# Strassen's seven products for the outer products of the second layer, with SiLU's values kept in float32

## The chip, the cores and the metric

The kernel runs on 1 core of one Trainium2 chip. The metric is the device time of one execution in microseconds; a version's time is the median of its runs. Engines are named as in the profile: PE is TensorE's matrix multiply and PEld its weight load, DVE is VectorE, ACT is ScalarE, POOL is GpSimd, SP is SyncE, which issues the DMAs here.

## The reference, cut to what matters

An attention stage (4 batches, 8 heads, pooled queries) gives x with 2304 rows (tokens) and 512 columns. Two layers follow, one behind the other:

```python
h = x @ w_in                # 2304x512 @ 512x2048
g = h * np.cos(h)
x = g @ w_out               # 2304x2048 @ 2048x512
h = x @ w_in2
g = h * (1.0 / (1.0 + np.exp(-h)))
out = g @ w_out2            # float32, the output
```

The attention's inputs are float32, the weights of both layers float64. This case is about the second layer, and in it about `g @ w_out2`.

## The kernel before, in words

Every product is made in float16 with a high and a low part of each operand: hi·hi, hi·lo and lo·hi are summed in PSUM, so a product of float32 quality costs three matmuls. Matmuls are at most 128 by 128 of weights by 512 columns.

**Tokens.** The second layer works on nine blocks of 256 tokens (`NB = 2 * B + 1`), a block's values lying as 128 partitions (a sixteenth of d_ff) by 256 tokens. `NF` is 16, the number of such slices f.

**First product of a block** (`g1_unit`, L527): for each f, 12 matmuls of 128x256 into half a PSUM bank; two f share a bank `h`, and there are two such banks. `g1_evac` (L540, ACT) takes two f at once out of PSUM with SiLU into `hk`, a float32 tile of four f with two buffers. After each fourth f, `g_silu` (L574, L575, DVE) scales `hk` and splits it into `gt`, float16 high and low. Four `gt` tiles, in the room of the first layer's weights, allow for four blocks (`TAIL_G`).

**Second product** (`g2_unit2`, L607): tokens are the stationary operand, 128 at a time; the weights' 512 columns stream. For each f there are 6 matmuls of 128x512: two halves of the block by three terms. So a block has 96 of them, in two banks `o0` and `o1`. `y_evac2` (L617, DVE) multiplies both banks by the scales into `osb`, and SP writes the rows out (L622).

**Order.** The program text issues the first product of blocks 0 to 2 alone, and from block 3 on one f of the first product, then one f of the second product of three blocks before. Behind the last first product, three blocks of second products remain. A planner puts the instructions of each engine in order before the run, by the text's order and by what its own timeline takes to be ready; it may bring later work forward where an engine would be idle.

**Weights.** `weight_steps` handles w_in2 and w_out2 as eight pieces each. A piece is loaded in three buffers (L177, SP), its float64 words are made into float32 (L206 to L218; ACT, DVE), a scale is found over the partitions with a tiny matmul on PE (L96), and the piece is split into high and low (L238, L239 on ACT, L240 on POOL). Three pieces of w_out2 are split before the second layer begins and five in its first 45 us. The POOL part of such a piece is one subtraction of 128x1024.

The blocks of the second layer are loaded (L871), measured and split (L890, L891) one ahead; they too find their scale with the matmul at L96, which has two PSUM buffers in `ps_m`.

Of the kernel before, what the change touches and what calls it, by code (L numbers as in the profile page):

```python
# [11 lines left out]
F32 = mybir.dt.float32  # L12
# [28 lines left out]
GT = 3  # L41
TAIL_G = 4


@with_exitstack
def attention_moe_moe_kernel(ctx, tc, q, k, v, w_in1, w_out1, w_in2, w_out2, out):
# [83 lines left out]
    def run_all(g):  # L130
        for _ in g:
            pass
# [10 lines left out]

    def new_w(tag, npc):
        w = Weights()
        w.npc = npc
        w.half = False
        for nm in ("si", "ui", "so", "uo"):
            setattr(w, nm, const.tile([128, npc], F32, name=nm + tag))
        w.uoT = const.tile([128, NC], F32, name="uoT" + tag)  # L150
        w.kg = const.tile([128, 1], F32, name="kg" + tag)
        w.ug = const.tile([128, 1], F32, name="ug" + tag)
        return w

    def weight_steps(w, srcs, stage, pspool, eng, nsub, bufs, ahead, wt_bufs=WT_BUFS):
# [16 lines left out]
        def more():  # L172
            if todo:
                kind, p, h = todo.pop(0)
                c, n = shape(kind)
                st = stage.tile([128, c, n, z], I32 if wide else F32, tag="wst", name="wst", bufs=bufs)
# [14 lines left out]
        def decode(kind, p):  # L191
            c, n = shape(kind)
            s, u = (w.si, w.ui) if kind == "i" else (w.so, w.uo)
            s, u = s[:, p:p + 1], u[:, p:p + 1]
            m = small.tile([128, nsub], F32, name="wm", tag="wm", bufs=3)
            sts = [staged.pop(0) for _ in range(nsub)]
            ts = []
            for h, st in enumerate(sts):
                if not wide:
                    ts.append(st[:, :, :, 0])  # L200
                    absmax(m[:, h:h + 1], ts[-1], AX.XY)
                    yield
                    continue
                t = stage.tile([128, c, n], F32, tag="wt", name="wt", bufs=wt_bufs)
# [16 lines left out]
                ts.append(st.bitcast(F32)[:, :, :, 1])  # L221
# [5 lines left out]
            for _ in early(scale_steps(m1, pspool(), (s, u), 14, wide), P_CH):  # L227
                pass
            decoded.append(ts)
            yield  # L230

        def write(kind, p):
            c, n = shape(kind)
            hw, lw = (w.ih, w.il) if kind == "i" else (w.oh, w.ol)
# [8 lines left out]
            if (kind, p) == ("i", npc - 1):  # L243
# [3 lines left out]
                nc.vector.tensor_reduce(out=w.ug, in_=w.ui, axis=AX.X, op=ALU.max)  # L247
                nc.vector.tensor_scalar(out=w.kg, in0=w.kg, scalar1=2.0**-15, scalar2=None, op0=ALU.mult)
                nc.vector.tensor_scalar(out=w.ug, in0=w.ug, scalar1=2.0**12, scalar2=None, op0=ALU.mult)

# [6 lines left out]

        r = npc // NC
        for e in range(r):
# [273 lines left out]
    def g1_evac(mp, w, blk, f, first):  # L533
        if f % 2 == 0:
            return
        g = f * w.npc // NF
        if f % 4 == 1:
            blk.hk = mp.p.tile([128, 4, GW], F32, tag="hk", name="hk", bufs=NB_HK)
        o = blk.hk[:, (f % 4) - 1:(f % 4) + 1, :]
        nc.scalar.activation(  # L540
# [58 lines left out]

    def g2_unit2(w, blk, f, pool):  # L600

        if f == 0:
            blk.y = [pool.tile([128, DM], F32, tag="o%d" % i, name="o") for i in range(2)]
        gh, gl = blk.g[f // 4]
        for i in range(2):
            for e, (gt, wt) in enumerate(((gh, w.oh), (gh, w.ol), (gl, w.oh))):
                nc.tensor.matmul(  # L607
                    blk.y[i], gt[:, f % 4, i * 128:(i + 1) * 128], wt[:, f, :],
                    start=(f == 0 and e == 0), stop=(f == NF - 1 and e == 2),
                )  # L610

    def y_evac2(W2, pool, blk, dsts):
        cy = y_scale(W2, blk.u, W2.uo, "cy0")
        for i in range(2):
            o = pool.tile([128, DM], F32, tag="x32_%d" % i, name="osb")
            np_ = W2.npc
            nc.vector.tensor_tensor(  # L617
                out=o.rearrange("p (c n) -> p c n", c=np_), in0=blk.y[i].rearrange("p (c n) -> p c n", c=np_),
                in1=cy.rearrange("p (c n) -> p c n", n=1).to_broadcast([128, np_, DM // np_]), op=ALU.mult,
            )  # L620
            for dst, p0, n in dsts[i]:
                nc.sync.dma_start(out=dst, in_=o[p0:p0 + n, :])  # L622


    if True:
        W1 = new_w("1", 8)
        alloc_w(W1, wpool, "1")
        ydr = [dram.tile([128, NC * GW], F32, name="ydr%d" % i) for i in range(2 * B + 1)]
        xrem = wpool.tile([128, B, NP * D], F32, name="xrem")

# [10 lines left out]
        state.psw = ps_h  # L641
        W2 = new_w("2", 8)
        state.credit = 0.0
# [148 lines left out]
        for n, (b, j) in enumerate(pairs):  # L792
# [13 lines left out]
            else:  # L806
                at.src_stack.close()
                w2st = moe_stack.enter_context(tc.tile_pool(name="w2st", bufs=1, reuse_waits="tile"))
                wgen2 = weight_steps(W2, (w_in2, w_out2), w2st, lambda: state.psw, nc.sync, 1, W2_BUFS, 1, 1)
# [52 lines left out]

        alloc_w(W2, w2p, "2")
        state.psw = ps_m
# [32 lines left out]
        def y_consts(yb):  # L897
            yb.blk.c = x_scale_consts(W2, yb.s, yb.u, False)
            yb.blk.u = yb.u
            yb.blk.gt = wpool.tile([128, 2, NF, GW], F16, tag=("ih1", "il1", "oh1", "ol1")[yb.n % TAIL_G], name="gt", bufs=1)  # L900

# [6 lines left out]
        while not W2.half:  # L908
            next(wgen2)

        def out_dst(n):
# [13 lines left out]
        cur = yb.blk  # L925
        pend = []

        def second():
            blk, ff, nn = pend.pop(0)
            g2_unit2(W2, blk, ff, ps_o)  # L930
            if ff == NF - 1:
                y_evac2(W2, wpool, blk, out_dst(nn))

        gen = None
        for n in range(NB):
            nyb = y_load(n + 1) if n + 1 < NB else None
            gen = y_split(nyb) if nyb else None
            for f in range(NF):
                g1_unit(W2, cur, f)
                g1_evac(state.mp, W2, cur, f, False)  # L940
                if f % 4 == 3:
                    g_silu(cur, f)
                pend.append((cur, f, n))
# [3 lines left out]
                if len(pend) > (TAIL_G - 1) * NF:  # L947
                    second()
            if n == TAIL_G - 2:
                run_all(wgen2)  # L950
            if gen is not None:
                run_all(gen)
            if nyb:
                y_consts(nyb)
                cur = nyb.blk
        while pend:
            second()
        ctx.enter_context(moe_stack)
# [30 lines left out]
```

## Time and profile before

| | us |
|---|---|
| median of 3 runs | 1407.86 (1405.83 to 1409.97) |
| the profiled execution's own time | 1411.62 |
| its span, first to last instruction | 1409.8 |
| second layer, first matmul to last matmul | 1021.0 to 1404.6 |

The profile has a page (busy time per engine, 40 slices of the span, the chain that ended last, groups of instructions) and a trace that can be asked for any stretch. In a group's row, "x36 | 46.2, 1282 | 0.9" means 36 instructions, 46.2 us busy in sum, 1282 ns mean, and 0.9 us that the engine sat idle just before them. Matmuls are pipelined: the mean of one is longer than the distance from one to the next, so the pace is read from runs of them in the chain.

### The profile page before, as it was taken

The page shows a single profiled execution, that of the slowest core. Times are in us where ns is not written, and L with a number is a line of the kernel's source. Part 1 is how long each engine was busy: PE and PEld are TensorE (multiplying, and loading weights), DVE is VectorE, ACT ScalarE, POOL GpSimd, SP SyncE. Part 2 cuts the span into 40 slices and gives each one's busy share as a digit, 9 for nine tenths or more (in the row PEclk, how much of TensorE's full clock was granted, in tenths as well). Part 3 has the DMA queues.
Part 4 walks back from the last instruction along what each step waited for, and adds up shares of the span by engine and source line. Part 5 has one row for each costly group of instructions (what it writes and reads, how often), then busy time and mean ns, then how long its engine had stood idle before and what let it go on. Part 6 is the DMA issues. An engine that isn't in the chain of part 4 may idle for free.

```text
span 1409.8 us, 24849 instructions
## 1 busy us (share of the span) xinstructions
PE 1162.9 (82%) x10020; PEld 852.0 (60%) x10020; DVE 996.4 (71%) x1848; ACT 767.5 (54%) x907; POOL 567.2 (40%) x296
## 2 busy tenths in 40 slices
PE   1465356787988778898889889979989999999998
PEld 0243233475676556666667678868878766666643
DVE  7999997778777888977999885997776323223110
ACT  3686487668777678876788775553363111111100
POOL 1577276535755466645666563552321000000000
PEclk9976568699999989998999999999999999999999
DMA  7799789987799999978899964441330000000001
GB/s 232 192 239 209 188 155 204 202 171 135 154 201 174 202 194 211 177 151 181 152 209 184 214 131 91 151 119 46 90 105 32 16 31 30 16 16 16 1 30 30
DMA packets 493074, 186.16 MB, mean 132 GB/s; under 512 B 433056, under 2 KB 467872, under 8 KB 492960
## 3 DMA queue, kind: packets, MB, share of 16 engines
q1 hardware_dynamic: 492960, 184.59, 61.7%
q8 instruction: 78, 1.28, 0.4%
q14 instruction: 36, 0.29, 0.1%
HBM read 66.58 MB, written 9.44 MB: 54 GB/s over the span
## 4 chain that ended last, share of the span: by engine, by line
PE 36%; DVE 25%; ACT 9%; issue 8%; DMA 7%; POOL 2%; SPq 2%; ACTq 0%; DVEq 0%; POOLq 0%
PE h L527 14%; PE o L607 13%; DVE sc L410 5%; PE y L586 5%; DMA hlT<-hl 3%; DVE tt L553 2%; DVE tt L552 2%; POOL hl L429 2%; PE sp L391 2%; ACT hl L424 2%; SPq L431 2%; PE pv L442 2%; DVE gh L567 1%; DVE tt L562 1%; DVE vt L311 1%
## 5 line engine op out<-in xcount | busy, mean ns | idle before, releaser
L429 POOL TENSOR_TENSOR hl<-sc,hl 128x1152 f16<-128x1152 f32 x144 | 367.8, 2563 | 189.9 <-ACT hl L424 110.8
L391 PE MATMUL sp<-kT,qT 128*128 128x512 f16 (+1 forms) x768 | 197.6, 375 | 111.2 <-DVE sc L410 86.5
L527 PEld LDWEIGHTS <-ih 128*128 128x128 f16 x2304 | 225.8, 99 | 64.6 <-issue 12.5
L410 DVE TENSOR_SCALAR_CACHE_REDUCE sc<-sp,psu 128x512 f32<-128x512 f32 (+1 forms) x288 | 229.2, 807 | 40.2 <-PE sp L391 38.8
L540 ACT ACTIVATE hk<-h,ca 128x512 f32<-128x512 f32 x144 | 97.7, 682 | 255.0 <-PE h L527 251.0
L418 ACT ACTIVATE sc<-sc,nb 128x1152 f32<-128x1152 f32 x144 | 180.3, 1252 | 95.2 <-DVE nb L415 80.6
L442 PE MATMUL pv<-vt,hlT 128*128 128x130 f16 (+1 forms) x1440 | 197.2, 239 | 39.6 <-DMA hlT<-hl 33.3
L527 PE MATMUL h<-ys,ih 128*128 128x256 f16 x1152 | 194.8, 273 | 2.9 <-ACT hk L540 2.7
L442 PEld LDWEIGHTS <-hlT 128*128 128x128 f16 (+1 forms) x1440 | 148.6, 111 | 71.0 <-DMA hlT<-hl 45.4
L527 PE MATMUL h<-xT,ih 128*128 128x256 f16 x1024 | 187.1, 276 | 4.7 <-ACT hk L540 3.9
L446 PE MATMUL pv<-vt,hlT 128*128 128x65 f16 (+1 forms) x1440 | 189.5, 209 | 0.0
L607 PE MATMUL o<-oh,gt 128*128 128x512 f16 x576 | 187.9, 379 | 1.0 <-ACT oh L238 0.6
L391 PEld LDWEIGHTS <-qT 128*128 128x128 f16 x768 | 77.9, 110 | 179.2 <-issue 137.1
L424 ACT ACTIVATE hl<-sc 128x1152 f16<-128x1152 f32 x144 | 165.5, 1157 | 18.5 <-DMA xT<-xn 8.9
L586 PE MATMUL y<-gl,oh 128*128 128x256 f16 x576 | 159.4, 277 | 3.7 <-POOL gl L568 3.7
L586 PE MATMUL y<-gh,oh 128*128 128x256 f16 x576 | 159.8, 277 | 2.5 <-ACT y L595 1.7
L586 PE MATMUL y<-gh,ol 128*128 128x256 f16 x576 | 159.7, 277 | 0.0
L527 PE MATMUL h<-ys,il 128*128 128x256 f16 x576 | 157.0, 273 | 0.0
L446 PEld LDWEIGHTS <-hlT 128*128 128x128 f16 (+1 forms) x1440 | 143.7, 108 | 16.2 <-issue 6.7
L527 PE MATMUL h<-xT,il 128*128 128x256 f16 x512 | 141.5, 276 | 0.0
L568 POOL TENSOR_TENSOR gl<-tt,gh 128x1024 f16<-128x1024 f32 x36 | 93.5, 2598 | 110.2 <-DVE gh L567 105.5
L607 PEld LDWEIGHTS <-gt 128*128 128x128 f16 x864 | 84.6, 98 | 81.3 <-issue 2.1
(281 smaller groups left out, 1884.5 us busy)
## 6 DMA issues: line engine op xcount, KB each, us to landing
wst<-in_moe_w_in_dram SPq DMA_DIRECT2D x16, 1024.0 KB, 5.7
wst<-in_moe_w_out_dram SPq DMA_DIRECT2D x16, 1024.0 KB, 6.2
stk<-in_k_dram SPq DMA_DIRECT2D x32, 288.0 KB, 4.0
stv<-in_v_dram SPq DMA_DIRECT2D x32, 288.0 KB, 4.4
stq<-in_q_dram SPq DMA_DIRECT2D x32, 256.0 KB, 3.1
ydr<-y SPq DMA_DIRECT2D x9, 512.0 KB, 3.8
y32b<-ydr SPq DMA_DIRECT2D x9, 512.0 KB, 3.3
out_dram<-osb SPq DMA_DIRECT2D x16, 256.0 KB, 2.1
```

The costliest lines, as they stand in the source:

```text
L391: nc.tensor.matmul(sp[:, o - a:o - a + n], P.qT[e][:, t, :], kT[:, o:o + n], start=(e == 0), stop=(e == 1))
L410: nc.vector.tensor_scalar(out=T.sc[:, a:z], in0=sp, scalar1=T.P.su, scalar2=None, op0=ALU.mult, op1=ALU.min, accum_out=mx[:, x:x + 1],)
L418: nc.scalar.activation(out=T.sc, in_=T.sc, func=AF.Exp, scale=-1.0, bias=nb)
L424: nc.scalar.activation(out=hi, in_=T.sc, func=AF.Copy)
L429: nc.gpsimd.tensor_tensor(out=T.hl[:, 1, :], in0=T.sc, in1=T.hl[:, 0, :], op=ALU.subtract)
L442: nc.tensor.matmul(G.pv[r, T.gi], T.hlT[:, 0, c, r], P.vt[i][:, c], start=(c == 0), stop=(c == KC - 1), skip_group_check=True,)
L446: nc.tensor.matmul(G.pv[r, T.gi, 0], T.hlT[:, 1, c, r], P.vt[i][:, c, 0], start=False, stop=(c == KC - 1), skip_group_check=True,)
L527: nc.tensor.matmul(hp, wt[:, c, f * 128:(f + 1) * 128], xt(c), start=(i == 0), stop=(i == 3 * NC - 1), skip_group_check=True,)
L540: nc.scalar.activation(out=o, in_=blk.hp, func=AF.Copy if first else AF.Silu, scale=blk.c.a[:, g:g + 1])
L568: nc.gpsimd.tensor_tensor(out=G.gl, in0=t, in1=gh, op=ALU.subtract)
L586: nc.tensor.matmul(blk.y[:, oc, :], wt[:, f, oc * 128:(oc + 1) * 128], gt[:, f % 4, :], start=(f == 0 and e == 0 and oc % 2 == 0), stop=(f ...
L607: nc.tensor.matmul(blk.y[i], gt[:, f % 4, i * 128:(i + 1) * 128], wt[:, f, :], start=(f == 0 and e == 0), stop=(f == NF - 1 and e == 2),)
```

## The change

- The second product of a block is no longer six matmuls per f, but seven products of quarters (Strassen's scheme in Winograd's form). The block's values are cut in halves of d_ff and halves of tokens (a11, a12, a21, a22), the weights in halves of d_ff and halves of d_model (b11 and so on). A quarter product has 8 slices by 3 terms, with weights of 256 columns.
- SiLU writes float32 values straight into one of four slots that hold a whole block; `g_silu` is gone. `outer_operand` makes the sums of quarters in place on DVE and splits each of the seven left operands: high part on ACT, low part on DVE. There are seven buffers for them, and the text prepares five ahead. One slot in four is made of smaller tiles, and is handled in pieces of 4 or 2 slices.
- The sums of the weights' quarters are made on POOL (`write_sums`) when a piece is split: four subtractions of 128x256, then the seven high parts (ACT) and low parts (POOL). A piece of w_out2 is loaded by two DMAs with rows half as long.
- Partial results leave PSUM after most products: copies on ACT, additions and scalings on DVE, into a float32 tile `o` of the block. Three kinds of PSUM banks are used: Y (two, alternating by block), X and W. The scale matmul's bank `ps_m` has one buffer instead of two.
- `outer_steps` issues half a product at a time, from block 3, f = 8 on, 14 half products for 16 f. What remains is issued after the last first product.
- The copies into `uoT` (L261) are no longer made for the second layer.

The diff, cut to its core:

```diff
+G2_AT, OP_AHEAD = 8, 5
...
+        def halves(ops, t, p):
...
+                nc.scalar.activation(out=h, in_=tt, func=AF.Copy)
+                nc.gpsimd.tensor_tensor(out=l, in0=tt, in1=h, op=ALU.subtract)
+
+        def write_sums(p):
+            st = decoded.pop(0)[0]
+            v, f = (st[:, :, :, z] for z in (1, 0))
+            nc.scalar.activation(out=v, in_=v, func=AF.Copy, scale=w.so[:, p:p + 1])
...
+            for o, x, y in ((t1, b12, b11), (t3, b22, b12), (t2, b22, t1), (t4, b21, t2)):
+                nc.gpsimd.tensor_tensor(out=o, in0=x, in1=y, op=ALU.subtract)
+            halves((0, 2), v[:, 0:NF], p)
+            yield
+            halves((2, 1), b22, p)
+            halves((3, 4), f, p)
+            more()
+            yield
...
-        r = npc // NC
+        r = 0 if w.sums else npc // NC
...
+            o = blk.view(f - 1, 2)
...
-    def g_silu(blk, f):
-        hk = blk.hk
-        gh, gl = (blk.gt[:, e, f - 3:f + 1, :] for e in range(2))
-        nc.vector.tensor_scalar(out=gh, in0=hk, scalar1=blk.c.k, scalar2=None, op0=ALU.mult)
-        nc.vector.scalar_tensor_tensor(out=gl, in0=hk, scalar=blk.c.k, in1=gh, op0=ALU.mult, op1=ALU.subtract)
-        blk.g.append((gh, gl))
...
+    PRODUCTS = ("a11", "a12", "s2", "s1", "s3", "a22", "s4")
...
+        if op == "s2":
+            s1 = mp.p.tile([128, HF, 128], F32, tag="hk", name="s1", bufs=NB_HK)
+            blk.s1 = lambda c, n: s1[:, c:c + n, :]
+            total(blk.s1, a22, a21, ALU.add, g1)
+            total(a21, a11, a21, ALU.subtract, g0)
+            total(a11, blk.s1, a11, ALU.subtract, g0)
+        elif op == "s4":
+            total(a12, a12, a11, ALU.subtract, g1)
...
+        t = opp.tile([128, 2, HF, 128], F16, tag="op", name="op", bufs=len(PRODUCTS))
+        for c in range(0, HF, g):
+            h, l = t[:, 0, c:c + g, :], t[:, 1, c:c + g, :]
+            nc.scalar.activation(out=h, in_=x(c, g), func=AF.Copy, scale=blk.c.k)
+            nc.vector.scalar_tensor_tensor(
+                out=l, in0=x(c, g), scalar=blk.c.k, in1=h, op0=ALU.mult, op1=ALU.subtract
+            )
...
+        seq = [(0, "a11")]
+        for n in range(len(blocks)):
+            seq += [(n, op) for op in ("a12", "s2", "s1", "s3")]
+            if n + 1 < len(blocks):
+                seq.append((n + 1, "a11"))
+            seq += [(n, "a22"), (n, "s4")]
...
+            for c in range(HF):
+                for e, wt in ((0, oh), (0, ol), (1, oh)):
+                    nc.tensor.matmul(bank, t[:, e, c, :], wt[:, c, :], start=start, stop=True, skip_group_check=True)
+                    start = False
+                if c == HF // 2 - 1:
+                    yield
+            o = B.o
+            if op == "a11":
+                copy(o[:, 0, d0], bank)
+            elif op == "a12":
+                add(o[:, 0, d0], bank)
+            elif op == "s2":
+                copy(o[:, 0, d1], bank)
+            elif op == "s3":
+                copy(o[:, 1, d1], bank)
+                add(o[:, 1, d1], B.W)
+            elif op == "a22":
+                scaled(B, o[:, 1, d0], bank)
+                scaled(B, o[:, 1, d1], o[:, 1, d1])
+            elif op == "s4":
+                add(o[:, 0, d1], bank)
+                for d in (d0, d1):
+                    scaled(B, o[:, 0, d], o[:, 0, d])
...
-        ps_m = ctx.enter_context(tc.tile_pool(name="ps_m", bufs=2, space=PSUM, side="right"))
+        ps_m = ctx.enter_context(tc.tile_pool(name="ps_m", bufs=1, space=PSUM, side="right"))
...
+                if outer is None and n == TAIL_G - 1 and f == G2_AT:
+                    outer = outer_steps(state.mp, opp, W2, blocks, banks, out_dst, OP_AHEAD)
+                if outer is not None:
+                    credit += 14
+                    while credit >= NF:
+                        credit -= NF
+                        next(outer, None)
...
-        while pend:
-            second()
+        run_all(outer)
```

## Rows read from the trace of the kernel before

**Rows 1.** The page, part 1: busy time of each engine over the span.

```profile
PE 1162.9 (82%) x10020; PEld 852.0 (60%) x10020; DVE 996.4 (71%) x1848; ACT 767.5 (54%) x907; POOL 567.2 (40%) x296
```

**Rows 2.** The page, part 2: 40 slices, busy tenths of PE and POOL.

```profile
PE   1465356787988778898889889979989999999998
...
POOL 1577276535755466645666563552321000000000
```

**Rows 3.** Stretches of the second layer: length, busy PE, PEld, DVE, ACT, POOL; granted clock, DMA.

```profile
1021.00:1064.30 43.30, 37.74 (x340) 32.95 (x339) 33.85 (x63) 25.16 (x31) 10.62 (x4) 1.00 0.31 96
1064.30:1098.60 34.30, 34.30 (x296) 28.89 (x296) 18.28 (x22) 10.78 (x15) 2.12 (x1) 1.00 0.06 20
1098.60:1341.70 243.10, 242.97 (x1685) 164.41 (x1684) 67.63 (x96) 37.51 (x52) 0.00 (x0) 1.00 0.05 18
1341.70:1404.60 62.90, 62.63 (x288) 28.05 (x287) 5.88 (x9) 0.00 (x0) 0.00 (x0) 1.00 0.07 26
```

**Rows 4.** The chain that ended last, by time: start, length, engine, line, count.

```profile
1098.59 1.31 PE h L527 x12
1099.90 1.30 PE o L607 x6
...
1341.69 20.25 PE o L607 x93
...
1383.72 20.89 PE o L607 x96
```

**Rows 5.** Groups of instructions from 1000 us to the end.

```profile
L527 PE MATMUL h<-ys,ih 128*128 128x256 f16 x1142 | 193.1, 273 | 2.9 <-ACT hk L540 2.7
L607 PE MATMUL o<-oh,gt 128*128 128x512 f16 x576 | 187.9, 379 | 1.0 <-ACT oh L238 0.6
L527 PEld LDWEIGHTS <-ih 128*128 128x128 f16 x1142 | 111.8, 98 | 38.7 <-issue 4.0
L607 PEld LDWEIGHTS <-gt 128*128 128x128 f16 x864 | 84.6, 98 | 81.3 <-issue 2.1
L540 ACT ACTIVATE hk<-h,ca 128x512 f32<-128x512 f32 x72 | 49.2, 686 | 233.9 <-PE h L527 229.9 <-issue 3.9
L575 DVE SCALAR_TENSOR_TENSOR gt<-hk,ck,gt 128x1024 f16<-128x1024 f32 x36 | 46.2, 1282 | 0.9
L574 DVE TENSOR_SCALAR gt<-hk,ck 128x1024 f16<-128x1024 f32 x36 | 28.4, 788 | 120.7 <-ACT hk L540 120.7
L617 DVE TENSOR_TENSOR osb<-o,cy 128x512 f32<-128x512 f32 x18 | 12.3, 689 | 106.7 <-PE o L607 106.7
L239 ACT ACTIVATE wst<-wst,so 128x1024 f32<-128x1024 f32 x6 | 7.4, 1239 | 0.0
L218 DVE SCALAR_TENSOR_TENSOR wst<-wst 128x1024 int32<-128x1024 int32 x4 | 4.9, 1223 | 0.0
L595 ACT ACTIVATE y<-y,cy 128x256 f32<-128x256 f32 x4 | 1.6, 475 | 5.2 <-PE y L586 5.2
```

**Rows 6.** PE in order of time, 1040 to 1080 us: the matmuls with a wait.

```profile
1044.09 0.38 PE L527 MATMUL h<-ys,ih 128*128 128x256 f16 x2 [1.11 <-ACT hk L540]
...
1057.54 0.38 PE L96 MATMUL bm<-mw,mean 128*128 128x1 f32 x2 [2.01 <-DVE mw L91]
...
1064.27 0.59 PE L607 MATMUL o<-oh,gt 128*128 128x512 f16 x2 [0.63 <-ACT oh L238]
```

**Rows 7.** POOL's split of w_out2 (busy time by stretch), and one of them in time.

```profile
1021.00:1070.00 49.00, 12.74 (x5) 1.00 0.28 87
...
1031.92 2.12 POOL L240 TENSOR_TENSOR ol<-wst,oh 128x1024 f16<-128x1024 f32 x1 [18.19 <-ACT wst L239]
...
1057.69 3.06 POOL L240 TENSOR_TENSOR ol<-wst,oh 128x1024 f16<-128x1024 f32 x1 [10.89 <-ACT wst L239]
```

**Rows 8.** DVE in order of time: the same instruction beside POOL's split and without it.

```profile
1032.45 2.14 DVE L574 TENSOR_SCALAR gt<-hk,ck 128x1024 f16<-128x1024 f32 x1 [0.81 <-ACT hk L540]
...
1040.19 0.75 DVE L574 TENSOR_SCALAR gt<-hk,ck 128x1024 f16<-128x1024 f32 x1 [2.70 <-ACT hk L540]
```

**Rows 9.** DMA issues from 900 to 1110 us: count, KB each, us to landing.

```profile
wst<-in_moe_w_out_dram SPq DMA_DIRECT2D x8, 1024.0 KB, 6.1
```

**Rows 10.** The end in order of time, all engines.

```profile
1403.99 1.34 DVE L617 TENSOR_TENSOR osb<-o,cy 128x512 f32<-128x512 f32 x2 [19.68 <-PE o L607]
```

More of the change, by code (lines that the diff above doesn't have):

```diff
@@ L147, in new_w @@
         w.half = False
+        w.sums = sums
         for nm in ("si", "ui", "so", "uo"):
@@ L175, in more @@
                 c, n = shape(kind)
-                st = stage.tile([128, c, n, z], I32 if wide else F32, tag="wst", name="wst", bufs=bufs)
+                dt = I32 if wide else F32
+                if w.sums and kind == "o":
+                    n //= 2
+                    st = stage.tile([128, 2, c, n, z], dt, tag="wst", name="wst", bufs=bufs)
+                    for j in range(2):
+                        o = j * (DM // 2) + p * n
+                        eng.dma_start(
+                            out=st[:, j].rearrange("p c f z -> p c (f z)"),
+                            in_=srcs[1][:, o * z:(o + n) * z].rearrange("(c p) f -> p c f", p=128),
+                        )
+                    staged.append(st.rearrange("p j c f z -> p (j c) f z"))
+                    return
+                st = stage.tile([128, c, n, z], dt, tag="wst", name="wst", bufs=bufs)
                 eng.dma_start(
@@ L220, in decode @@
                 )
-                ts.append(st.bitcast(F32)[:, :, :, 1])
+                ts.append(st.bitcast(F32) if w.sums and kind == "o" else st.bitcast(F32)[:, :, :, 1])
                 yield
@@ L226, in decode @@
                 nc.vector.tensor_reduce(out=m1, in_=m, axis=AX.X, op=ALU.max)
-            for _ in early(scale_steps(m1, pspool(), (s, u), 14, wide), P_CH):
+            for _ in early(scale_steps(m1, pspool(), (s, u), 13 if w.sums and kind == "o" else 14, wide), P_CH):
                 pass
@@ L598, in y_evac1 @@
         nc.sync.dma_start(out=ydst, in_=y32.rearrange("p c n -> p (c n)"))
[L600 to L616, printed above, removed]
+    class Slot:
+        def __init__(self, parts):
+            self.parts = parts
+        def view(self, c, n):
+            for c0, n0, t in self.parts:
+                if c0 <= c and c + n <= c0 + n0:
+                    return t[:, c - c0:c - c0 + n, :]
+    HF = NF // 2
+    PRODUCTS = ("a11", "a12", "s2", "s1", "s3", "a22", "s4")
@@ new lines, in outer_steps, with prepare, copy, add @@
+    def outer_steps(mp, opp, w, blocks, banks, dsts, ahead_n):
+        seq = [(0, "a11")]
[4 more added lines that the diff above has]
+            seq += [(n, "a22"), (n, "s4")]
+        todo = list(seq)
+        ready = []
+        def prepare(k):
+            while todo and len(ready) < k:
+                n, op = todo[0]
+                if blocks[n] is None:
+                    return
+                todo.pop(0)
+                ready.append(outer_operand(mp, opp, blocks[n], op))
+        def copy(o, x):
+            nc.scalar.activation(out=o, in_=x, func=AF.Copy)
+        def add(o, x):
+            nc.vector.tensor_tensor(out=o, in0=o, in1=x, op=ALU.add)
+        def scaled(B, o, x):
+            np_ = w.npc
@@ new lines, in outer_steps @@
+        d0, d1 = slice(0, DM // 2), slice(DM // 2, DM)
+        for n, op in seq:
+            prepare(ahead_n)
+            B = blocks[n]
+            t = ready.pop(0)
+            if op == "a11":
+                B.Y = banks("Y", n)
+                B.o = (opp, wpool)[n % 2].tile([128, 2, DM], F32, tag=("osb", "xrem")[n % 2], name="osb", bufs=1)
+                B.cy = y_scale(w, B.u, w.uo, "cy0")
+            elif op == "a12":
+                B.X = banks("X", n)
+            elif op == "s1":
+                B.W = banks("W", n)
+            bank = B.X if op == "a12" else B.W if op in ("s1", "s4") else B.Y
+            start = op in ("a11", "a12", "s1")
+            i = OUTER[op]
+            oh, ol = next((h[:, i - x0], l[:, i - x0]) for x0, x1, h, l in w.ops if x0 <= i < x1)
+            for c in range(HF):
[5 more added lines that the diff above has]
+            o = B.o
+            if op == "a11":
+                copy(o[:, 0, d0], bank)
+            elif op == "a12":
+                add(o[:, 0, d0], bank)
[11 more added lines that the diff above has]
+                    scaled(B, o[:, 0, d], o[:, 0, d])
+                for i in range(2):
+                    for dst, p0, m in dsts(n)[i]:
+                        nc.sync.dma_start(out=dst, in_=o[p0:p0 + m, i, :])
+            yield
@@ L898, in y_consts @@
             yb.blk.c = x_scale_consts(W2, yb.s, yb.u, False)
-            yb.blk.u = yb.u
-            yb.blk.gt = wpool.tile([128, 2, NF, GW], F16, tag=("ih1", "il1", "oh1", "ol1")[yb.n % TAIL_G], name="gt", bufs=1)
+            blk = yb.blk
+            blk.u = yb.u
+            k = yb.n % TAIL_G
+            if k < 3:
+                t = wpool.tile([128, NF, GW], F32, tag=("il1", "oh1", "ol1")[k], name="gs", bufs=1)
+                blk.view = Slot([(0, NF, t)]).view
+                blk.grain = (HF, HF)
+            else:
+                parts = [(4 * j, 4, wpool.tile([128, 4, GW], F32, tag="x32_%d" % j, name="gs")) for j in range(2)]
+                parts += [
+                    (HF + 2 * j, 2, state.mp.p.tile([128, 2, GW], F32, tag=nm, name="gs", bufs=NB_G))
+                    for j, nm in enumerate(("gh", "gl", "gh", "gl"))
+                ]
+                blk.view = Slot(parts).view
+                blk.grain = (4, 2)
         yb = y_load(0)
@@ L925, in attention_moe_moe_kernel, with banks @@
         cur = yb.blk
[L926 to L934, printed above, removed]
+        blocks = [None] * NB
+        def banks(nm, n):
+            if nm == "Y":
+                t = ps_o.tile([128, DM], F32, tag="o%d" % (n % 2), name="oy")
+            elif nm == "X":
+                t = ps_y.tile([128, NC, GW], F32, tag="y", name="ox").rearrange("p c n -> p (c n)")
+            else:
+                t = ps_m.tile([128, DM], F32, tag="w", name="ow")
+            return t[:, 0:DM // 2]
+        outer = None
+        credit = 0
         for n in range(NB):
```

72 lines of the change are left out of this document (52 added, 20 removed).

## The prediction

> **What bounds the kernel now.** I read the page first. Over the whole span PE is the busiest engine, at 82% [rows 1], but that share is a mean over unlike stages. The slices show that the last quarter is another regime: PE stands at nine tenths and more, and POOL is empty [rows 2]. The change touches this quarter, so I cut the second layer into four stretches [rows 3]. From 1064.3 us to the last matmul at 1404.6 PE is busy without a hole, at a granted clock of 1.00, while DVE is busy 67.6 of 243.1 us and ACT 37.5 in the third stretch. The chain that ended last says the same: from 1098.6 us on it is 12 matmuls of the first product, 6 of the second, and so on, and then second products alone [rows 4]. Only the first stretch has gaps.
>
> The pace: 12 matmuls of 256 columns take 1.31 us, 0.1092 each; of a block's 96 with 512 columns the last starts 20.89 − 0.38 us behind the first, 0.2159 each [rows 4] (0.38 is the mean of one [rows 5]). Half the columns cost half the time. The second layer needs 1728 × 0.1092 + 864 × 0.2159 = 188.7 + 186.5 = 375.2 us in the 383.6 us between 1021.0 and 1404.6, so 8.4 us are idle, all in the first stretch: the waits marked there are for ACT's SiLU, the scale matmul and a weight's high part [rows 6].
>
> **The change, part by part.**
>
> *Matmuls.* A block needs 7 products × 8 slices × 3 terms = 168 matmuls of 256 columns, 168 × 0.1092 = 18.35 us, instead of 96 × 0.2159 = 20.73 us. Nine blocks: 9 × 2.38 = **21.4 us saved**, on the engine that sets the end. Each matmul loads its own weights before and after; a load takes 98 ns in both products [rows 5], and hides under 109 ns as it does in the first product now.
>
> Here a rule speaks against the change. The rows give 109 and 216 ns for 256 and 512 columns. The Trainium skill, page "TensorE: Matmul & The Clock Gate", section "Back-to-back issue gap", states for pairs of load and matmul in a real kernel about 81 ns at 128 columns and 131 at 512; on a straight line 256 columns would take about 98, an estimate. By it a block would go from 12.6 to 16.5 us, and nine blocks would lose 35 us. The trace does not agree: its 512 columns take 216 ns. I take the rows.
>
> *DVE.* `g_silu` goes: 36 × (1.28 + 0.79) us [rows 5], none of it on PE's path after the first stretch. New for each block are four sums of 1024 elements and seven low parts. No float32 sum of two SBUF tiles by DVE stands in the rows; the nearest two-input instruction, L218, has 1.22, half that (a copy at L574's rate, 0.79, lies between) is the lower bound and L575's 1.28 the upper. I take 1.22. Low parts are L575's form, 1.28. Seven reads of 256 columns out of PSUM: L617 has 0.69 for 512, so between 0.34 and 0.69; ACT's for 256 is 0.48 [rows 5]; I take 0.45. Sum: 4.9 + 9.0 + 3.2 = 17.1 us per block. While both products run, a block lasts 16 × 1.31 + 18.35 = 39.3 us of PE, which covers it. In the drain behind the last first product the cover is 18.35 us: thin, and see the second rival.
>
> *ACT.* Seven high parts at 1.24 (L239) and three copies at 0.48, 10.1 us per block, beside SiLU's 8 × 0.69. Covered both times.
>
> *The drain's length.* From block 3, f = 8 on there are 88 slices with 14/16 half products each: 77 of 126. So 24.5 products, 64.2 us, follow the last first product, about as the 62.9 us of three blocks now, the fourth stretch [rows 3].
>
> *Weights.* POOL's work per piece grows from 1024 to 1024 + 512 + 256 + 1024 = 2816 elements: 2.55 us [rows 7] becomes 7.0, with the seven further instructions at nothing (lower bound) or at a small instruction's 0.1 to 0.2 us each (up to 8.4). The five pieces inside the second layer now end before 1070 us [rows 7]; five times 4.5 us more gives 1092. The first quarter product comes after 3.5 blocks of first products, 1021.0 + 56 × 1.31 + 8.4 = 1102.8. So this costs **nothing, with 11 us of cover**; gone that, PE waits us for us. The DMAs: eight more issues on SP, and rows of half the length, between 6.1 [rows 9] and 12.2 us to landing; three buffers load ahead, and behind them on SP stand block loads that are one block early. Nothing.
>
> POOL holds up DVE: the same instruction took 2.14 us when POOL's split (1031.92 to 1034.04 [rows 7]) ran at its start, and 0.75 alone [rows 8]. The skill, page "SBUF — State Buffer", section "Who interferes with whom", calls this an exclusive lock of a shared port pair; by it DVE could lose all of POOL's added 22 us in this stretch. That alone would not reach PE. DVE loses `g_silu` there (8 × 2.07 = 16.6 us of its 33.9), and SiLU no longer waits for it. So I leave the 8.4 us of idle as they are; the bounds are all gone (−8.4) and as much again (+8.4).
>
> *One scale buffer instead of two* (L96): a second scale matmul waits until DVE has read the first. Between nothing and the 2.0 us that PE once waits for such a scale [rows 6], twice at most; I take 0.5.
>
> *Ends.* At the first quarter product PE may wait for SiLU, a high and a low part: 0 to 0.69 + 1.24 + 1.28 = 3.2; the planner issues first products meanwhile; 0.5. In the last block nothing stands between s3 and a22, so PE waits for the copy of Y: 0.48 and signalling, 0.7. After the last matmul DVE has now 0.69 twice [rows 10]; then one addition and one or two scalings of 256, about 0.3 more.
>
> *Sum:* −21.4 + 0.5 + 0.5 + 0.7 + 0.3 = **−19.4 us**. Against the profiled execution 1411.6 − 19.4 = 1392.2. That execution stands 3.8 us above the median of 1407.9, so the median becomes **1388.5**.
>
> **The rivals.**
>
> *SiLU stuck behind operand splits (slower).* ACT works in its queue's order. If SiLU stands behind the high parts of s2, s1 and s3, it waits for three sums on DVE (3.7) and three high parts (3.7). If those sums stand behind an addition that waits for a product still on PE, 2.6 more: 10.0 us. PE has two `h` banks, and fills a pair in 2 × 1.31 + 1.75 × 1.31 = 4.9 us, so it bears 4.9 − 0.7 = 4.2. Up to 5.8 us a block in 5.5 shared blocks = 32: **1420**. It decides from 4.3 us a block (23.6 in all). For: the sums are new in front of ACT, which till now waited for PE alone (230 us of L540's idle [rows 5]). Against: the planner orders by readiness, and sums may run seven buffers ahead. With the sums unhindered it is 7.4 − 4.2 = 3.2 a block, 18 us: **1406**, no difference.
>
> *The drain is bound by DVE and ACT.* If high part and DVE work alternate without overlap, a product takes 1.24 + 17.1/7 = 3.7 us against PE's 2.62. Five are ready at its start: 19.5 × 3.7 + 2.6 = 74.8 instead of 64.2: +10.6, **1399**. For: slot 7 is done in small pieces, some 20 DVE instructions more. Against: that needs no overlap at all.
>
> *The first stretch closes.* SiLU no longer waits for `hk`'s release: −8.4, **1380**. Against: two of its three marked waits are for scales and weights.
>
> *Weights late.* If load (12.2) and POOL (7.0) of a piece follow one another, five take 96 us from 1030: 1126, 23 past their time: **1412**. Three buffers speak against it.
>
> *The change does not do what it says (slower):* 256 columns with the new operands, of which two matmuls in three share their left operand, are slower than 0.109 us. Each 0.01 us more costs 1512 × 0.01 = 15 us, and at 0.1234 (20.73/168) nothing is won. A load wholly uncovered (0.098 + 0.109) is the upper end; at 0.130 the time is 1388.5 + 31 = **1420**. Against: the rows' 0.109, in this very stage and with a load for each matmul. The skill's page on TensorE, cited above, would have it so in another way, by cheaper matmuls of 512 columns; its estimate is 1407.9 + 35 = 1443.
>
> **How the numbers follow.** Chances: forecast 0.63, first stretch closes 0.11, drain 0.12, SiLU stuck 0.05 (and 0.04 for its mild form), weights late 0.03, slow matmuls 0.02. Of that last chance the page's rule has half. The three runs spread over 4 us, 0.3%, which is about what a measurement can tell from no change. Faster: 0.63 + 0.11 + 0.12 = 0.86; same: 0.07; slower: 0.07. The range reaches from the closed stretch, 1380, to the bound drain, 1399, and holds 0.86; I keep it there for the idle's upper bound.
>
> **What would show it.** Right: L607's groups give way to 1512 matmuls of 256 columns at 0.109 us; PE stays full from about 1064 us on; last matmul near 1385; POOL's work on w_out2 ends before 1100. Wrong: idle of PE ahead of SiLU's banks in each block; PE waiting for the low part of an operand in the drain; a hole near 1100 that ends with POOL; or blocks in the drain that last longer than 18.4 us. If the matmuls run at more than 0.115, the sum itself falls.

## The result, and the profile after

| | before | after |
|---|---|---|
| median, us (4 runs each) | 1407.46 | 1399.17 (1395.71 to 1399.74) |
| profiled execution: span, us | 1409.8 | 1396.6 |
| first layer's last matmul starts, us | 1020.9 | 1020.2 |
| last matmul ends, us | 1404.6 | 1391.9 |
| between the two, us | 383.7 | 371.7 |

The ratio is **0.9918, with a 95% interval of 0.9890 to 0.9947**: 11.5 us faster (8.3 between the two medians), where 19.4 were forecast. That is the forecast side. The range reached from 1380 to 1399: the median, 1399.17, lies on its upper edge, the ratio's 0.9918 × 1407.46 = 1395.9 just inside. In the profiled executions the second layer became 12.0 us shorter, and its end after the last matmul 0.5 us (4.7 instead of 5.2).

The stretches of the second layer after the change, cut at its own landmarks; columns as in [rows 3]:

```profile
1020.30:1062.00 41.70, 40.70 (x376) 36.22 (x374) 18.12 (x35) 24.95 (x38) 23.62 (x24) 1.00 0.43 99
1062.00:1079.50 17.50, 6.03 (x30) 3.98 (x28) 16.47 (x23) 8.54 (x11) 10.91 (x9) 0.61 0.32 68
1079.50:1099.80 20.30, 19.54 (x179) 17.11 (x177) 11.97 (x23) 12.42 (x19) 17.36 (x16) 1.00 0.08 27
1099.80:1325.80 226.00, 226.00 (x2073) 202.39 (x2071) 117.11 (x164) 92.88 (x127) 0.00 (x0) 1.00 0.06 20
1325.80:1391.90 66.10, 65.62 (x600) 58.42 (x598) 41.97 (x66) 26.51 (x42) 0.00 (x0) 1.00 0.08 28
```

From 1099.8 us on all is as the sum had it: PE is full, and 2073 matmuls in 226.0 us are 0.109 us each. The drain (last line) is PE's too, with DVE busy 42.0 of 66.1 us. One line is foreign: between 1062.0 and 1079.5 us PE has 30 matmuls in 17.5 us, at a granted clock of 0.61. Before the change no stretch was like it.

The groups that take the place of L607 and `g_silu` in [rows 5], from 1000 us to the end:

```profile
L742 PEld LDWEIGHTS <-op 128*128 128x128 f16 x1512 | 147.9, 98 | 18.0 <-issue 0.6 <-DVE op L685 0.2 <-ACT op L684 0.2
...
L742 PE MATMUL oy<-ops,op 128*128 128x256 f16 x864 | 103.0, 273 | 0.5 <-ACT osb L711 0.5
...
L258 POOL TENSOR_TENSOR ops<-wst,ops 128x512 f16<-128x512 f32 (+1 forms) x27 | 33.4, 1256 | 2.5 <-ACT ops L257 2.5
...
L267 POOL TENSOR_TENSOR wst<-wst 128x256 f32<-128x256 f32 x26 | 26.3, 1027 | 28.1 <-ACT wst L263 28.1
...
L685 DVE SCALAR_TENSOR_TENSOR op<-s,ck,op 128x1024 f16<-128x1024 f32 x9 | 11.5, 1283 | 25.2 <-ACT op L684 25.2
...
L684 ACT ACTIVATE op<-s,ck 128x1024 f16<-128x1024 f32 x9 | 10.3, 1146 | 7.3 <-PE ow L742 7.3
...
L714 DVE TENSOR_TENSOR osb<-osb,ow 128x256 f32<-128x256 f32 x18 | 7.6, 420 | 33.8 <-PE ow L742 22.7 <-ACT osb L711 10.9
```

There are the 1512 loads and matmuls; the matmuls of bank Y waited 0.5 us in all for a copy, and the loads next to nothing for operands. POOL's work per piece of w_out2 is four times 1.03 and four times 1.26 us, 9.1 us, where 7.0 to 8.4 had been worked out.

The hole itself: PE in order of time, the rows with a wait and the first rows behind them.

```profile
1061.76 0.28 PE L97 MATMUL bm<-ym,mean 128*128 128x1 f32 x2
...
1062.01 0.27 PE L573 MATMUL h<-ys,il 128*128 128x256 f16 x1
1068.44 0.59 PE L97 MATMUL bm<-mw,mean 128*128 128x1 f32 x2 [6.17 <-DVE mw L92]
1068.90 0.59 PE L573 MATMUL h<-ys,ih 128*128 128x256 f16 x2
1074.79 0.37 PE L573 MATMUL h<-ys,ih 128*128 128x256 f16 x1 [5.30 <-DVE ys L1037]
1074.95 0.42 PE L573 MATMUL h<-ys,il 128*128 128x256 f16 x1
1075.17 0.63 PE L573 MATMUL h<-ys,ih 128*128 128x256 f16 x2
...
1079.01 0.58 PE L573 MATMUL h<-ys,ih 128*128 128x256 f16 x2
1079.42 0.27 PE L573 MATMUL h<-ys,il 128*128 128x256 f16 x1
```

PE stands 6.2 us before the scale matmul of a weight piece (`mw`), then 5.3 us before block 2's first matmul, whose split `ys` is late. Behind that, 256 columns go at 0.215 us instead of 0.109 until 1079.4 us: the granted clock is at the lower of its two levels, 1.2 GHz. It fell inside the first wait, while PE had nothing to do; two stretches of that wait show it (columns as in [rows 3], the third number from the end is the clock):

```profile
1064.00:1065.00 1.00, 0.00 (x0) 0.00 (x0) 1.00 (x4) 0.97 (x3) 0.82 (x2) 1.00 1.34 212
1066.00:1067.00 1.00, 0.00 (x0) 0.00 (x0) 1.00 (x1) 1.00 (x2) 1.00 (x2) 0.50 0.00 0
```

It was back at 1.00 from 1079.4 us on. That costs about (1079.4 − 1075.0)/2 = 2.2 us more. Together 13.7 us.

Why both were late is in the chain of the changed kernel, in order of time:

```profile
1050.36 1.61 POOL wst L267 x2
1051.97 2.23 POOL ops L258 x2
...
1054.22 0.37 SPq L184
...
1054.64 7.14 DMA wst<-in_moe_w_out_dram
...
1061.88 1.13 ACT wt L220
...
1063.03 1.23 DVE wt L221 x2
...
1065.69 1.66 DVE wst L229
...
1067.42 0.97 DVE mw L92
...
1072.89 1.85 DVE ys L1037
```

POOL frees a weight buffer at 1054.2; only then is the next piece loaded; its words become float32 on ACT and DVE; and its scale matmul had been put in PE's queue at a place that PE reached at 1062. The rows half as long are not what made it late: over all loads of w_out2 the median to landing was 6.2 us, 6.1 before [rows 9]. Some DVE instructions take longer than alone while POOL works beside them. `mw` (L92) is the plainest: 128x1 elements, the first row from the hole, the second from the piece decoded without POOL's work beside it.

```profile
1067.34 1.05 DVE L92 SCALAR_TENSOR_TENSOR mw<-wm,mw 128x1 int32<-128x1 int32 x1
```

```profile
1058.90 0.15 DVE L92 SCALAR_TENSOR_TENSOR mw<-wm,mw 128x1 int32<-128x1 int32 x1
```

POOL's `L258` ran from 1066.23 to 1068.37, so the first ended with it. The Trainium skill, page "SBUF — State Buffer", section "Who interferes with whom", says that a VectorE instruction with two SBUF inputs contends with a GpSimd instruction that reads SBUF, for a port pair that is an exclusive lock; these two rows agree. It is a part only: L224, L229 and L92 lost about 2 us of the 6.2.

And block 2? Its maximum was known early, its scale came late:

```profile
1028.40 1.21 DVE L113 TENSOR_REDUCE ym<-y32b 128x1 f32<-128x1024 f32 x1
...
1060.17 0.15 DVE L100 TENSOR_SCALAR uo<-bm 128x1 f32<-128x1 f32 x1
```

The maximum is there at 1029.6 us. Its scale matmul runs at 1061.76, 32 us later, behind that of a weight piece, which DVE read out of the one scale bank at 1060.17. Before, with two banks, the two ran next to each other, and PE did not wait for block 2's split at all:

```profile
1049.33 0.28 PE L96 MATMUL bm<-mw,mean 128*128 128x1 f32 x2
1049.47 0.36 PE L96 MATMUL bm<-ym,mean 128*128 128x1 f32 x2
```

The late piece holds block 2 up a second time, in DVE's queue. DVE read block 2's scale at 1064.2 us, but ended its split only at 1074.7: between them stood the late piece's L224, L229, L92 and L232 (5.7 us) and one sum of values (L667, 1.8 us).

### The profile page after: what moved, and what is told of

Same layout as the page of the kernel before. It is cut to its first block, busy times and chain, and to the rows that moved or that the text cites. A ratio compares the mean times of both kernels' runs of the same rounds, so it can differ in the third digit from the quotient of the medians.

```text
span 1396.6 us, 26497 instructions
## 1 busy us (share of the span) xinstructions
PE 1140.9 (82%) x10668; PEld 915.4 (66%) x10668; DVE 1057.2 (76%) x1958; ACT 857.6 (61%) x1045; POOL 620.8 (44%) x352
## 5 line engine op out<-in xcount | busy, mean ns | idle before, releaser
L437 PE MATMUL sp<-kT,qT 128*128 128x512 f16 (+1 forms) x768 | 193.7, 369 | 109.5 <-DVE sc L456 82.5
L573 PE MATMUL h<-xT,ih 128*128 128x256 f16 x1024 | 191.3, 280 | 3.8 <-ACT hk L589 2.7
L488 PEld LDWEIGHTS <-hlT 128*128 128x128 f16 (+1 forms) x1440 | 146.4, 110 | 72.1 <-DMA hlT<-hl 46.8
L742 PEld LDWEIGHTS <-op 128*128 128x128 f16 x1512 | 147.9, 98 | 18.0 <-issue 0.6
L492 PEld LDWEIGHTS <-hlT 128*128 128x128 f16 (+1 forms) x1440 | 142.1, 108 | 16.2 <-issue 6.5
L573 PEld LDWEIGHTS <-il 128*128 128x128 f16 x1152 | 114.5, 99 | 22.6 <-issue 7.1
L628 PEld LDWEIGHTS <-oh 128*128 128x128 f16 x1152 | 113.3, 100 | 23.1 <-issue 6.0
```

What stands on the lines that cost most here:

```text
L437: nc.tensor.matmul(sp[:, o - a:o - a + n], P.qT[e][:, t, :], kT[:, o:o + n], start=(e == 0), stop=(e == 1))
L488: nc.tensor.matmul(G.pv[r, T.gi], T.hlT[:, 0, c, r], P.vt[i][:, c], start=(c == 0), stop=(c == KC - 1), skip_group_check=True,)
L492: nc.tensor.matmul(G.pv[r, T.gi, 0], T.hlT[:, 1, c, r], P.vt[i][:, c, 0], start=False, stop=(c == KC - 1), skip_group_check=True,)
L573: nc.tensor.matmul(hp, wt[:, c, f * 128:(f + 1) * 128], xt(c), start=(i == 0), stop=(i == 3 * NC - 1), skip_group_check=True,)
L628: nc.tensor.matmul(blk.y[:, oc, :], wt[:, f, oc * 128:(oc + 1) * 128], gt[:, f % 4, :], start=(f == 0 and e == 0 and oc % 2 == 0), stop=(f ...
L742: nc.tensor.matmul(bank, t[:, e, c, :], wt[:, c, :], start=start, stop=True, skip_group_check=True)
```

## The experiments

Three theories were set against each other. **A:** POOL's sums of weight quarters free the buffers late, and the late piece's scale holds up PE. **B:** the one scale bank puts block 2's scale behind the late piece. **C:** DVE's sums of values, which the planner brings forward into this stretch (two of 1.8 and 2.1 us in the hole), stand before block 2's split. The first layer ends up to 9 us earlier or later from profile to profile, so beside the ratio I give the time from the start of the first layer's last matmul to the end of the last matmul, which the profile has without that: 383.7 us before, 371.7 us after. It comes from one execution of each kernel; the changed kernel, which has two, shows 371.7 and 370.3. Ratios are to the kernel before on the same chip. The expectations that give times mean the first chip, where the kernel before took 1407.5 us; a ratio times 1407.5 is the time to hold against them.

**1. No sums of weights (e1_no_sums).**

```diff
-            for o, x, y in ((t1, b12, b11), (t3, b22, b12), (t2, b22, t1), (t4, b21, t2)):
-                nc.gpsimd.tensor_tensor(out=o, in0=x, in1=y, op=ALU.subtract)
...
-            halves((3, 4), f, p)
+            halves((3, 4), v, p)
```

> Leaves out the four subtractions of weight quarters on POOL for each piece of w_out2 (the split then takes plain quarters in their place, so the output is not the reference's). Theory A (POOL's sums free the weights' buffers late, and the late piece's scale matmul, which stands in PE's queue, holds up the first product): the POOL work of a piece falls by about 3.4 us, the loads come earlier, both waits of the hole at 1062 to 1080 us shrink to under 2 us together and the clock does not fall: about 1388 us. Theory B (the single scale bank puts the scale of block 2 behind the late piece): the hole stays for the most part, 1395 to 1399. Theory C (the sums of values, brought forward on DVE, stand before block 2's split): the hole loses the 6.2 us wait for the weight's scale at most and keeps 5.3 us: 1392 to 1395.

Ratio 0.9819 (0.9773 to 0.9864), second layer 357.9 us. The stretch of the hole:

```profile
1062.00:1079.50 17.50, 16.69 (x151) 14.43 (x149) 16.05 (x35) 11.99 (x19) 11.85 (x9) 1.00 0.10 31
```

The hole is gone, and the clock stays at 1.00; in the whole second layer no wait of PE is longer than 0.8 us. POOL's sums are needed for the hole. That fits A, but B too, if lateness is what B needs. By the ratio the time is 1382.0 us, 6 below A's forecast.

**2. The sums on DVE (e2_dve_sums).**

```diff
-                nc.gpsimd.tensor_tensor(out=o, in0=x, in1=y, op=ALU.subtract)
+                nc.vector.tensor_tensor(out=o, in0=x, in1=y, op=ALU.subtract)
```

> The same four subtractions on DVE instead of POOL, nothing left out. Theory A: as without them, since DVE has room there (about 10 of 20 us busy before the hole) and four times 0.42 us are 1.7 us per piece: 1388 to 1391 us. Theory B: 1395 to 1399, hole still there. Theory C: DVE has more to do ahead of block 2's split, so the wait of 5.3 us grows: 1397 to 1402.

Ratio 0.9873 (0.9839 to 0.9907), second layer 364.1 us. The median subtraction took 0.42 us on DVE, 0.85 on POOL. The longest waits that are left are 2.1 us for SiLU at 1055 us and 1.8 us for block 2's split:

```profile
1072.16 0.27 PE L573 MATMUL h<-ys,ih 128*128 128x256 f16 x1 [1.78 <-DVE ys L1037]
```

Block 2's scale matmul still ran as late as 1061.8 us, but PE waited 1.8 us for the split instead of 5.3, and for no weight piece. By the ratio the time is 1389.6 us, as A had it. C's forecast, a longer wait for the split, failed.

**3. The first sum of values kept out of this stretch (e4_s1_late).**

```diff
-            s1 = mp.p.tile([128, HF, 128], F32, tag="hk", name="s1", bufs=NB_HK)
+            s1 = opp.tile([128, HF, 128], F32, tag="s1", name="s1", bufs=1)
...
-        t = opp.tile([128, 2, HF, 128], F16, tag="op", name="op", bufs=len(PRODUCTS))
+        t = opp.tile([128, 2, HF, 128], F16, tag="op", name="op", bufs=6)
```

> The tile of the first sum of values (s1) is taken from the operands' room, which comes free only when the weights' staging is closed, so DVE's sums of values cannot be brought forward into the weights' stretch; operand buffers six instead of seven. Theory C: the 5.3 us wait for block 2's split shrinks to under 2 us, about 1395 us or less. Theories A and B: those sums cost DVE at most 2 x 1.8 us in the hole; time within 2 us of the changed kernel's 1398, the wait of 6.2 us for the weight's scale unchanged. Six buffers instead of seven cost nothing by all three.

Ratio 0.9910 (0.9878 to 0.9942), second layer 370.9 us. PE's waits in the stretch:

```profile
1073.31 0.58 PE L97 MATMUL bm<-mw,mean 128*128 128x1 f32 x2 [5.16 <-DVE mw L92]
...
1077.87 0.37 PE L573 MATMUL h<-ys,ih 128*128 128x256 f16 x1 [3.54 <-DVE ys L1037]
```

No sum of values ran on DVE between 1065 and 1080 us, and the hole stands: 8.7 us of waits instead of 11.5. C falls as the cause: it had the second wait under 2 us. The time does not decide here (by the ratio 1394.8 us, which C had forecast too), the trace does. The second wait is 1.8 us shorter than in the changed kernel, as long as the one sum that stood before block 2's split.

**4. Two banks for the scales (e6_two_banks).** Blocks 0 to 3 use a bank that the second product needs only later.

```diff
+        ps_yb = type("B", (), {"tile": lambda self, *a, **k: ps_o.tile([128, DM], F32, tag="o1", name="bm").rearrange("p (a b) -> p a b", a=2)})()
...
-            yield from early(scale_steps(m, ps_m, (yb.s, yb.u), 14), P_CH)
+            yield from early(scale_steps(m, ps_yb if yb.n <= 3 else ps_m, (yb.s, yb.u), 14), P_CH)
```

> The scales of blocks 0 to 3 of the second layer use the bank that block 1's Y will use later, so weights and blocks no longer share one scale bank; nothing else is changed. Theory B: block 2's scale is found soon after its maximum (1035 us), the wait of 5.3 us for its split is gone; if the late piece's matmul then stands behind enough first products, the 6.2 us are gone too: 1386 to 1392 us. Theory A: block 2's wait may go, but the late piece's scale still holds PE for about 6 us somewhere before 1090 us: 1392 to 1395. Theory C: the split is still late behind the sums, 1395 to 1398.

Ratio 0.9860 (0.9824 to 0.9896), second layer 363.7 us, 8 us shorter than with one bank. PE's waits from 1060 to 1075 us:

```profile
1062.16 0.38 PE L97 MATMUL bm<-mw,mean 128*128 128x1 f32 x2 [0.87 <-DVE mw L92]
1069.12 0.38 PE L97 MATMUL bm<-mw,mean 128*128 128x1 f32 x2 [1.09 <-DVE mw L92]
1070.45 0.38 PE L573 MATMUL h<-ys,ih 128*128 128x256 f16 x2 [0.49 <-ACT gs L589]
1074.02 0.38 PE L573 MATMUL h<-ys,ih 128*128 128x256 f16 x2 [0.68 <-ACT gs L589]
```

POOL's work is unchanged, yet both long waits are gone: block 2's scale ran at 1032.7 us, and the planner, which now has another order to lay out, put the late pieces' scales where they are about 1 us late each. B's forecast came true, by the ratio with 1387.8 us. That block 2's scale ran at 1032.7 also shows that its maximum was there before 1035 us, the time which the expectation gives; at 1035 DVE worked on block 3's. A's remnant of 6 us did not show as one wait, though pieces still are a little late (2.6 us in sum).

**5. One bank in the kernel before (e8_before_one_bank).**

```diff
-        ps_m = ctx.enter_context(tc.tile_pool(name="ps_m", bufs=2, space=PSUM, side="right"))
+        ps_m = ctx.enter_context(tc.tile_pool(name="ps_m", bufs=1, space=PSUM, side="right"))
```

> The kernel before with one scale bank instead of two, nothing else changed. If the single bank costs by itself (theory B alone), PE gets a hole before 1070 us of 8 to 12 us and the time rises by as much, ratio 1.006 to 1.009. If it costs only together with late pieces (POOL's sums, theory A with B), the pieces here are on time and the time rises by 0 to 3 us, ratio 1.000 to 1.002.

Ratio 0.9985 (0.9963 to 1.0007), second layer 381.4 us. Block 2's scale and PE's longest wait:

```profile
1056.07 0.28 PE L96 MATMUL bm<-ym,mean 128*128 128x1 f32 x2
...
1064.51 0.27 PE L527 MATMUL h<-ys,ih 128*128 128x256 f16 x1 [2.51 <-DVE ys L891]
```

One bank puts block 2's scale late here too, 9.6 us later than with two, counted from the first layer's last matmul, and PE waits 2.5 us for block 2's split. But the other waits are shorter by as much (5.4 us in all, 5.3 with two banks), and the time does not rise. So neither POOL's sums with two banks (363.7) nor one bank without the sums on POOL (357.9 and 364.1, and 381.4 in the kernel before) makes the hole of two waits of over 5 us; only both together do (371.7, and 370.3 below).

**6. The same bank, another order (e11_late_scale).** The text issues a piece's scale two steps later.

```diff
-G2_AT, OP_AHEAD = 8, 5
+G2_AT, OP_AHEAD, LATE = 8, 5, 2
...
-                yield
+                yield from [None] * (1 + LATE * (w.sums and kind == "o" and p > 1))
```

> The changed kernel with its one scale bank and POOL's sums; only the text issues a w_out2 piece's scale two steps later (from the third piece on), by which block 2's scale takes the bank, and its place in PE's queue, ahead of the late pieces (14 slices into the second layer instead of 31.8). If the hole comes from the order in which the one bank is handed out (theory A with B), the 5.3 us wait for block 2's split goes, the late pieces' own waits fall below 3 us, the clock stays up, and the time comes close to two banks: ratio 0.985 to 0.988. If the number of banks or POOL's load alone were the cause, nothing changes: 0.990 to 0.993.

Second layer 364.1 us: the hole is gone with one bank and with POOL's sums. Block 2's scale ran at 1041.9 us; the late pieces' scales were waited for 0.2 us, and the longest wait left is 1.5 us, for a scale to be read out of the bank.

```profile
1041.90 0.28 PE L97 MATMUL bm<-ym,mean 128*128 128x1 f32 x2
...
1074.55 0.38 PE L97 MATMUL bm<-mw,mean 128*128 128x1 f32 x2 [0.24 <-DVE mw L92]
...
1080.29 0.38 PE L97 MATMUL bm<-ym,mean 128*128 128x1 f32 x2 [1.51 <-DVE uo L100]
```

The ratio, 0.9892 (0.9855 to 0.9930), does not tell it apart from the changed kernel by itself; the first layer ended at 1024.4 us in its profile, 4 us later than in the changed kernel's. So the trace decides here, not the time. The hole hangs on the order in which things are handed out, not on the number of banks alone. The edit moves a late piece's scale back in the bank's order and in PE's queue alike; which of the two does how much is not shown.

**7. Two operands ahead (e9_two_ahead),** on top of the two banks.

```diff
-G2_AT, OP_AHEAD = 8, 5
+G2_AT, OP_AHEAD = 8, 2
...
-        t = opp.tile([128, 2, HF, 128], F16, tag="op", name="op", bufs=len(PRODUCTS))
+        t = opp.tile([128, 2, HF, 128], F16, tag="op", name="op", bufs=2)
```

> The changed kernel with scale matmuls in two banks, and with operand buffers and preparation cut to two products instead of seven and five. If PE is full in the drain only because operands are ready long before (the lead covers DVE and ACT), the drain of 24.5 products grows from 64 us towards 24.5 x 3.7 = 91 us, and the shared blocks get waits: 10 to 30 us slower than with two banks alone (1392.8 in its runs). If DVE and ACT keep up with PE product by product, it is within 3 us of it.

Ratio 0.9874 (0.9833 to 0.9915), second layer 365.8 us against 363.7. Its drain, about 1318 to 1385 us:

```profile
1318.00:1385.00 67.00, 65.31 (x588) 56.54 (x585) 49.69 (x74) 31.35 (x45) 0.00 (x0) 1.00 0.08 28
```

PE loses under 2 us. DVE and ACT keep up with a lead of two operands; the lead of five to seven is comfort.

**8. Two banks and the sums on DVE (e7_dve_two):** the edits of 2 and 4 together.

> Two scale banks and the four subtractions of weight quarters on DVE instead of POOL. If the waits of about 1 us that are left with two banks come from POOL's pace (theory A), they go and the time falls by 2 to 4 us below two banks alone, ratio to the kernel before 0.983 to 0.985. If DVE's longer queue takes POOL's place (it had 61 of 80 us busy there with two banks), the time stays or rises by up to 3 us, ratio 0.986 to 0.988.

Ratio **0.9820 (0.9782 to 0.9859)**, median 1386.18 us beside 1413.75 on that chip: 25 us by the ratio. Second layer 359.5 us, of which 353.8 are matmuls: 4.2 us less than with two banks alone, so the waits that were left came in part from POOL's pace, as the first forecast had it. This is the best version of the study that computes the reference's result.

With it the four combinations are there. Second layer, and in brackets the sum of PE's waits in it, both in us:

| | one scale bank | two scale banks |
|---|---|---|
| sums on POOL | 371.7 and 370.3 (13.6 and 12.4) | 363.7 (7.5) |
| sums on DVE | 364.1 (6.9) | 359.5 (4.3) |

Against the lower right, one bank alone costs 4.6 us and POOL's sums alone 4.2. Both together cost 10.8 to 12.2, so 2.0 to 3.4 more than the sum of the two; the fallen clock, which only the hole brings, is 2.2 of it.

**9. The changed kernel again (e10_changed_again),** unchanged.

> The changed kernel as it is, beside the others on one chip, as their yardstick. Ratio 0.990 to 0.994, hole of about 11 us idle between 1060 and 1080 us, with the granted clock at half speed for some microseconds behind it.

Ratio 0.9904 (0.9872 to 0.9936), second layer 370.3 us. PE's two long waits:

```profile
1070.38 0.59 PE L97 MATMUL bm<-mw,mean 128*128 128x1 f32 x2 [5.09 <-DVE mw L92]
...
1076.72 0.37 PE L573 MATMUL h<-ys,ih 128*128 128x256 f16 x1 [5.31 <-DVE ys L1037]
```

So the hole is there in both profiled executions of the changed kernel.

## Why the prediction was right, and where it fell short

**Matmuls: right.** 24 matmuls of a product take 2.62 us (forecast 24 × 0.1092). The loads still took 98 ns. 1728 + 1512 matmuls need 353.8 us, 21.4 less than before. Without the hole (experiments 1, 2, 4, 6, 8) the second layer lost 20 to 26 us, so the 21.4 are there.

**The rule against the change: not borne out.** The Trainium skill, page "TensorE: Matmul & The Clock Gate", section "Back-to-back issue gap", has 131 ns for 512 columns, by which the change would have lost; the trace has 216 before, and 109 for 256 columns after.

**DVE and ACT: right.** A sum of 1024 alone took 1.22 us, the low part 1.28, a read of 256 out of PSUM 0.42 (taken: 0.45), a high part 1.15 (1.24), a copy 0.38 (0.48). Of the seven reads that the sum put down to PSUM three are of SBUF; they took 0.42 as well. In the drain DVE was busy 64% of the time. The rival "the drain is bound by DVE and ACT" falls by experiment 7 as well.

**SiLU stuck behind operand splits: did not happen.** From 1099.8 us to the last first product PE has no idle time.

**Ends: small.** The copy before a22 of the last block costs 0.5 us (forecast 0.7); the end after the last matmul is 0.5 us shorter, not 0.3 longer: the last block's lower half is scaled and sent out before the last product is done.

**The idle before: smaller than read.** Of the 8.4 us that the sum called idle, PE's waits were 5.3 (2.7 for SiLU, 2.0 for a scale, 0.6 for a weight's high part [rows 6]); scale matmuls make up most of the rest.

**Weights and the scale bank: the step that failed.** Two terms stood apart in the sum: "nothing, with 11 us of cover" for POOL's longer work, and 0.5 us for one scale bank, with the one wait of 2.0 us in [rows 6], "twice at most", as its bound. The first was measured against the wrong reader. For the first quarter product the cover held: POOL was done at 1097.6 us, and that product came at 1099.8. But each weight piece has an earlier reader on PE, its scale matmul, which stands in PE's queue among first products; a late piece stops them all. And the second term was priced as if pieces were in time. Together they cost 6.2 + 5.3 us, and 2.2 us more by the fallen clock, 13.7 in all. The rival "weights late" had the right picture, a load that follows POOL's work instead of running ahead, but held it against the first quarter product too.

Other waits shrank: the second layer's time without its matmuls was 8.5 us before (383.7 − 375.2) and 17.9 after (371.7 − 353.8), of which the hole has 13.7. So about half of what the rival "the first stretch closes" took came as well, and the net loss is 9.4 us, 7.7 more than the 1.7 forecast for waits. The end gave back 0.8. That makes 6.9 us short of the forecast in the profiled executions; by the ratio it is 7.9.

That the time still came out in the range is in part luck. Its upper end stood there for a drain bound by DVE and ACT, which did not come; the idle's upper bound, 8.4 us more for a DVE held up by POOL, is near the 9.4 that came, but by another path. Of the signs of being right, "PE stays full from about 1064 us on" failed, and the last matmul ended at 1391.9, not near 1385.

Two smaller errors lie in the same step. Six pieces instead of five were summed inside the second layer. And a piece took POOL 9.1 us instead of 7.0: four subtractions of 128x256 took 3.4 us at their median, one instruction of 128x1024 2.55 [rows 7], and POOL's instructions were longer beside DVE's, as DVE's were beside POOL's (L258 of 128x512 took 2.14 us at 1066.23, under DVE's L229, and 1.15 at 1096.47, with DVE idle).

Why the planner lays out such an order was not tried. Its timeline must have had the piece ready when PE came to it; that is argued from the order and not shown.

## What to carry to other kernels

When preparation work is made longer, look for all its readers on the bounding engine, not for the last: a tiny instruction in that engine's queue can hold everything behind it. Two cheap edits (one buffer less, a slower producer) can meet in one queue; price them together. Here each cost over 4 us alone, though one buffer less had cost nothing in the kernel before, and both cost 11 to 12. And look at the order in which a shared buffer is handed out before adding buffers: here issuing two steps later did as much as a second bank in the profiled second layer (364.1 and 363.7 us).

## What the hardware showed beyond what was expected

- The clock's cost: the granted clock fell to the lower level inside a wait of 6.2 us without a matmul and stayed there over a second one of 5.3 us; behind it 256 columns took 0.215 us each for 4.4 us. Waits of 11.5 us thus cost 13.7.
- A DVE instruction of one element per partition with two inputs (L92) took 1.05 us instead of 0.15 while POOL was at work. Its neighbours with one input (L104 at 1065.49, L108 at 1067.28) took 0.14 beside POOL's work.
- POOL's float32 subtraction of 128x256 took 0.85 us in the median, of 128x1024 into float16 2.55 us in the mean before [rows 7]; a quarter of the elements costs a third of the time. On DVE the same 128x256 took 0.42 us.
